# A fused attention and two-MLP kernel on one NeuronCore: first pair in native float32, shared transpose copies, sums on GpSimd, a new order

## The chip, the cores and the metric

The kernel runs on one core of a Trainium2 chip. The metric is the device time of one execution in microseconds (us), the median of several runs; lower is better. The engines are TensorE (PE for its matmuls, PEld for its weight loads), VectorE (DVE), ScalarE (ACT), GpSimd (POOL) and SyncE (SP, which issues every DMA of this kernel, in the order of its queue).

## What is computed

Block-causal attention over 4 batches, 8 heads, 576 positions and 64 columns a head; its output is the token matrix (2304 x 512) of two MLPs in a row.

```python
scores = scale * np.matmul(q, k.transpose(0, 1, 3, 2))
mask = block_i >= block_j            # blocks of 64 positions
attn = np.exp(scores - max); attn = attn / (sum + 1e-09)
x = np.matmul(attn, v)               # -> 2304 x 512
a = x @ w1;  b = x @ w2
x = (a * b @ w3) @ w_out             # 512 -> 1024 -> 1024 -> 512
h = x @ w_in                         # 512 -> 2048
out = np.where(h > 0, h, np.exp(np.minimum(h, 0)) - 1) @ w_out2
```

## The kernel before

**Precision.** Most matmuls run in three passes over operands that are split into a rounded part and a remainder (type fp32r; `PASSES` has the three combinations). A few run in native float32; the trace records each of these as two MATMUL rows. The weights come as 64-bit words, and `convert` makes float32 of each unit of 128 x 512 on ACT, DVE and POOL (L425 to L461), in four input buffers (`cr`).

**Stages.** First, attention for 16 pairs of heads (`attention(n, ...)`, n = 0 to 15) runs beside the product of w3 and w_out (`w_product`: 64 float32 matmuls `wps` of 128 x 512), which needs 24 converted units (`full`). Then `block2` multiplies the tokens with w1, w2 and that product (`a`, `b`, `y`); its matmuls mix with the attention of the later pairs. Last, `part_h` and `part_o` do the second MLP by a seven-product scheme (`hx hy hz`, `ox oy oz`); their weights come back from DRAM through a ring of three buffers `win` and one of four `wout`.

**One pair.** q and k are loaded into `raw` and split: ACT rounds (L570, L573), POOL and DVE make the remainders (L578, L583). For each of four groups of 128 queries (`group(g, seq)`) PE makes the scores `s` of both heads (L631, and L637 for the mask in the first four pairs), DVE takes the maxima (L652), ACT the exponentials with their sums (L657), PE transposes them into a bank `t` (L667), and ACT or DVE copies the bank to `pt` (`evac`, L521 or L522). `last_block` does the last 64 queries with a block-diagonal q (`qb`). `pv` multiplies with v (`o`, L757). `recip` adds up the sums and inverts them on DVE (L780 to L784); they go through DRAM (`scr`, `rr`) and POOL normalizes (L811). The score banks are 0, 1 and 2; `t` and `o` take turns in banks 3 and 4.

**Order.** `Plan.add` collects every operation with an engine, a guessed duration, a priority and its dependencies; `Plan.run` puts them in order by these guesses, and each engine then works through its list in that order. `TURNS` overrides the priority of some operations by their number. Until the first `wps` product, `filler` puts matmuls on a spare bank (`spare`, L1486) into gaps that the plan expects on PE.

Of the kernel before, what the change touches and what calls it, by code (L numbers as in the profile page):

```python
# [20 lines left out]
P = 128  # L21
WHOLE = 0
# [4 lines left out]
WO_PRIO = -3000.0  # L27
# [7 lines left out]
KP = 4  # L35
# [112 lines left out]
class Ring:  # L148
# [11 lines left out]
    def next(self):  # L160
        k = self.k % self.n
        self.k += 1
        self.last[k] = Buf(self.pool, self.tags[k], self.base, self.shape, self.dtype, self.last[k], self.gate)
        return self.last[k]
# [124 lines left out]
def attention_moe_moe2(  # L289
# [236 lines left out]
    def attention(n, first_op):  # L526
# [77 lines left out]
        def nm(c):  # L604
            return st()[:, c:c + 1]
# [938 lines left out]
```

## Time and profile before

| | before |
|---|---|
| median of 3 runs (lowest to highest) | 909.37 us (908.26 to 911.37) |
| the profiled execution: time, span | 908.46 us, 906.7 us |
| PE busy | 887.0 us (98%) |
| PEld busy | 785.4 us (87%) |
| DVE busy | 731.5 us (81%) |
| ACT busy | 504.9 us (56%) |
| POOL busy | 555.4 us (61%) |
| DMA | 186.15 MB, mean 205 GB/s |

The span runs from the first to the last instruction on the core; the 1.76 us between it and the execution's time lie outside. Matmuls are pipelined and their ends are modelled, so PE can count as busy while it makes less headway than it could.

### The profile page before, as it was taken

The numbers are of one execution on the slowest core, as the hardware profiler recorded it, in microseconds if no ns is written. First come the engines' busy times: TensorE is split into PE (matmuls) and PEld (weight loads), VectorE is DVE, ScalarE is ACT, GpSimd is POOL, SyncE is SP. The second block draws the span as 40 slices with busy tenths as digits, with TensorE's granted clock in tenths as the row PEclk, the third lists the DMA queues.
The fourth block names the chain that finished last, engine by engine and source line by source line (L and its number), as shares of the span: only waits on it lengthen the run. The fifth ranks groups of instructions, "written<-read, shape, count | busy, mean of one in ns | idle before, by whom it ended". The sixth has DMA issues, their size and how long they took to land.

```text
span 906.7 us, 15391 instructions
## 1 busy us (share of the span) xinstructions
PE 887.0 (98%) x5268; PEld 785.4 (87%) x5268; DVE 731.5 (81%) x1406; ACT 504.9 (56%) x1168; POOL 555.4 (61%) x529
## 2 busy tenths in 40 slices
PE   8899999999999999999999999999999999999998
PEld 3455568877788779999999999999999999999997
DVE  7998898798667675778898778788877788987896
ACT  6778876776556653435454554545634555444561
POOL 6666976454322223698898882138976178842796
PEclk9999999999999999999999999999999999999999
DMA  8765544554222105888567865877688776788666
GB/s 286 234 216 171 189 155 132 179 166 150 90 66 67 55 27 184 260 263 259 179 224 246 315 209 155 254 235 255 232 270 268 259 260 228 250 275 300 223 211 216
DMA packets 100750, 186.15 MB, mean 205 GB/s; under 512 B 8512, under 2 KB 50496, under 8 KB 100672
## 3 DMA queue, kind: packets, MB, share of 16 engines
q1 hardware_dynamic: 100672, 185.18, 61.8%
q8 instruction: 41, 0.67, 0.3%
q14 instruction: 37, 0.30, 0.1%
HBM read 147.85 MB, written 37.30 MB: 204 GB/s over the span
## 4 chain that ended last, share of the span: by engine, by line
PE 78%; DMA 8%; DVE 7%; POOL 2%; ACT 2%; issue 2%; SPq 1%; ACTq 0%; POOLq 0%; DVEq 0%
PE b L941 11%; PE a L941 10%; PE y L902 10%; PE hx L1192 8%; PE ox L1270 6%; PE hz L1192 5%; PE hy L1192 5%; PE o L757 4%; PE oz L1270 4%; PE oy L1270 4%; PE s L631 3%; PE t L667 3%; DMA win<-wsi 3%; PE wps L827 2%; DMA cr<-w 2%
## 5 line engine op out<-in xcount | busy, mean ns | idle before, releaser
L902 PE MATMUL y<-g,slab_lo 128*128 128x384 f32 x576 | 114.9, 340 | 0.4 <-DVE xy L925 0.3
L941 PE MATMUL b<-xs,slab_lo 128*128 128x384 f32 x576 | 111.3, 338 | 0.0
L941 PE MATMUL a<-xs,slab_lo 128*128 128x384 f32 x576 | 110.8, 337 | 0.0
L941 PEld LDWEIGHTS b<-xs,slab_lo 128*128 128x128 f32 x576 | 99.9, 188 | 0.7 <-DVE af L958 0.4
L941 PEld LDWEIGHTS a<-xs,slab_lo 128*128 128x128 f32 x576 | 99.9, 188 | 0.5 <-issue 0.5
L902 PEld LDWEIGHTS y<-g,slab_lo 128*128 128x128 f32 x576 | 99.0, 188 | 1.3 <-PE y L902 0.6
L1192 PE MATMUL hx<-sy,win 128*128 128x384 f32 x432 | 86.9, 335 | 0.1
L657 ACT ACTIVATE p<-s,st 128x256 f32<-128x256 f32 (+3 forms) x128 | 67.4, 529 | 29.0 <-DVE st L652 23.2
L1192 PEld LDWEIGHTS hx<-sy,win 128*128 128x128 f32 x432 | 75.7, 188 | 0.9 <-DVE ga L1074 0.4
L1270 PE MATMUL ox<-sp,wout 128*128 128x384 f32 x372 | 73.2, 334 | 0.0
L863 POOL TENSOR_TENSOR g<-af,g 128x384 fp32r<-128x384 f32 x48 | 53.8, 1125 | 26.4 <-ACT g L860 26.0
L652 DVE TENSOR_REDUCE st<-s 128x1 f32<-128x256 f32 (+3 forms) x128 | 61.6, 488 | 5.8 <-PE s L637 2.5
L1270 PEld LDWEIGHTS ox<-sp,wout 128*128 128x128 f32 x372 | 65.3, 188 | 0.0
L827 PE MATMUL wps<-full,full 128*128 128x512 f32 x128 | 60.8, 602 | 2.1 <-POOL full L455 1.9
L1192 PE MATMUL hz<-sy,win 128*128 128x384 f32 x288 | 58.0, 335 | 3.3 <-DMA win<-wsi 3.3
L1192 PE MATMUL hy<-sy,win 128*128 128x384 f32 x288 | 57.8, 335 | 0.2 <-DMA win<-wsi 0.2
L667 PE MATMUL t<-ident,p 128*128 128x128 f32 x320 | 54.3, 282 | 2.9 <-ACT p L657 2.0
L667 PEld LDWEIGHTS t<-ident,p 128*128 128x128 f32 x320 | 37.0, 140 | 22.5 <-ACT p L657 8.2
L432 ACT ACTIVATE ct<-cr 128x512 f32<-128x512 f32 x59 | 39.9, 677 | 29.4 <-POOL wt L455 13.6
L425 ACT ACTIVATE cr<-cr 128x512 int32<-128x512 uint32 x72 | 48.6, 681 | 11.9 <-DMA cr<-w 7.9
L1192 PEld LDWEIGHTS hz<-sy,win 128*128 128x128 f32 x288 | 50.4, 188 | 4.3 <-DMA win<-wsi 4.3
L757 PE MATMUL o<-pt,v 128*64 128x320 f32 (+4 forms) x448 | 52.7, 367 | 1.0 <-ACT pt L521 1.0
(175 smaller groups left out, 2135.1 us busy)
## 6 DMA issues: line engine op xcount, KB each, us to landing
wout<-wso SPq DMA_DIRECT2D x84, 512.0 KB
cr<-w SPq DMA_DIRECT2D x48, 512.0 KB
win<-wsi SPq DMA_DIRECT2D x24, 1024.0 KB
win<-wsi SPq DMA_DIRECT2D x24, 768.0 KB
cr<-w3T SPq DMA_DIRECT2D x16, 512.0 KB
wsi<-wh SPq DMA_DIRECT2D x8, 896.0 KB
wsi<-wt SPq DMA_DIRECT2D x8, 896.0 KB
wso<-wh SPq DMA_DIRECT2D x8, 896.0 KB
```

The lines of the kernel that those rows point to most:

```text
L425: nc.scalar.activation(out=low, in_=low.bitcast(U32), func=AF.Copy, scale=2.0**-29)
L432: nc.scalar.activation(out=t().bitcast(F32), in_=words()[1].bitcast(F32), func=AF.Abs)
L652: nc.vector.tensor_reduce(out=nm(c), in_=s()[:, 0:nk], axis=AX.X, op=ALU.max, negate=True)
L657: lambda s=s, c=c, p=p: nc.scalar.activation(out=p()[:, 0:nk], in_=s()[:, 0:nk], func=AF.Exp, bias=nm(c), scale=1.0, accum_out=sm(c)),
L667: nc.tensor.transpose(d[:, j, :], p()[:, j * P:(j + 1) * P], ident)
L757: nc.tensor.matmul(o()[D * h:D * h + D, lo:cols], lhsT=vt()[0:kn, j, D * h:D * h + D], rhs=p, start=(j == 0), stop=(j == last),)
L827: nc.tensor.matmul(ps(), lhsT=a[:, j, :], rhs=bb, start=(j == 0), stop=(j == KF - 1))
L863: lambda: nc.gpsimd.tensor_tensor(out=g()[:, 1, :], in0=src(), in1=g()[:, 0, :].bitcast(F32), op=ALU.subtract),
L902: nc.tensor.matmul(ps()[:, 0:T2], lhsT=w[:, a, n * P:(n + 1) * P], rhs=gs[m]()[:, c, :], start=(m == ms[0] and q == 0), stop=(m == ms[-1] ...
L941: nc.tensor.matmul(ps()[:, 0:T2], lhsT=w[:, a, u, k, :], rhs=xs()[:, k, c, :], start=(k == 0 and q == 0), stop=(k == KD - 1 and q == 2),)
L1192: nc.tensor.matmul(bk()[:, 0:T3], lhsT=w[:, a, k, :], rhs=s_(c), start=(first and k == 0 and i == 0), stop=(k == 1 and i == 2), skip_group ...
L1270: nc.tensor.matmul(to[n]()[:, 0:T3], lhsT=w[:, a, n * P:(n + 1) * P], rhs=sp(c), start=(first and q == 0 and i == 0), stop=(q == KP - 1 an ...
```

## The change

Five things change together.

1. `WHOLE` goes from 0 to 1: pair 0 is loaded straight into its q and k tiles in two column pieces (256 and 320), k is scaled piece by piece, and its scores are native float32 matmuls, one a head and group; its q for the last block has a buffer of its own, `qw`. It is also placed first on SP and PE, ahead of all weight products.
2. In groups 0 and 1 (`BOTH`) the transposes of the two heads go into one bank, and one copy moves both.
3. In `recip` the addition of the two last sums and of 1e-9 move from DVE to POOL, an operation of their own (`sums_of`) ahead of the reciprocal.
4. In the very last product of `part_o` the two halves of the output no longer alternate (`split_end`), and the filler before PE's first operation is counted at 0.45 us instead of 0.29 us.
5. `TURNS` is a new table, so the order changes on all engines throughout.

```diff
-WHOLE = 0
+WHOLE = 1
+BOTH = 2
-WO_PRIO = -3000.0
+WO_PRIO = -2499.995
...
-    4: -2505.56, 9: -100000.02, 22: -9857.07, 23: -997.98, 36: -3035.53, 41: -2498.87, 65: -2417.38, 69: -2499.99,
+    4: -10173.49, 5: -10172.92, 6: -10173.47, 7: -10173.5, 8: -2499.97, 24: -2452.67, 40: -9872.36, 56: -2400.0,
...
-                self.filler(int((t - free[e] - 0.6) / 0.29))
+                self.filler(int((t - free[e] - 0.6) / (0.29 if free[e] else 0.45)))
...
+        halves = (slice(0, 256), slice(256, S)) if whole else ()
...
+            for c, cs in enumerate(halves):
+                add(
+                    "SP", 0, lambda cs=cs: nc.sync.dma_start(out=f32(x, 0)[:, cs], in_=src[b, hp][:, cs]),
+                    w=[(x, 0, c)], prio=pr + 0.001 * c, nbytes=P * (cs.stop - cs.start) * 4,
+                )
...
+            if both:
+                t2 = turn("to", (3, 4), "t")
...
-                t = turn("to", (3, 4), "t")
+                t = t2 if both else turn("to", (3, 4), "t")
+                t0 = nk * h if both else 0
...
+                if both and h:
+                    evac(
+                        2 * nk, lambda pt=pt: pt()[:, :, 0:g + 1, q0:q0 + P],
+                        lambda t=t: t()[:, 0:2 * nk].rearrange("p (h j q) -> p h j q", h=2, q=P),
+                        [(t, 0), (t, 1)], [(pt, 0, g), (pt, 1, g)], pg,
+                    )
...
         def recip():
             a = st()
-            nc.vector.tensor_tensor(out=a[:, 16:17], in0=a[:, 16:17], in1=a[:, 21:22], op=ALU.add)
-            nc.vector.tensor_scalar_add(a[:, 12:21], a[:, 12:21], 1e-9)
             nc.vector.reciprocal(a[:, 32:41], a[:, 12:21])
...
+        def sums_of():
+            a = st()
+            nc.gpsimd.tensor_tensor(out=a[:, 16:17], in0=a[:, 16:17], in1=a[:, 21:22], op=ALU.add)
+            nc.gpsimd.tensor_scalar_add(a[:, 12:21], a[:, 12:21], 1e-9)
...
-                        prio=1e5 + 1000 * (j + 1) + 34 * (KP * x + q) + 17 * n, lag=LAG, kind="big",
+                        prio=1e5 + 1000 * (j + 1) + 34 * KP * x + (70 * n + 17 * q if split_end else 34 * q + 17 * n),
```

Three places show how the order moves. The first is the head of SP's queue, that is, what is loaded first. Before (`cr` are weights to convert, `raw` the q and k of a pair, `v` its values):

```order
L464 DMA cr_129<-wo 128x512
L464 DMA cr_131<-w3T 128x512
L464 DMA cr_129<-w3T 128x512
L464 DMA cr_131<-wo 128x512
L548 DMA v_145<-vt 128x4x128
L539 DMA raw_151<-kT 128x576
L539 DMA raw_151<-qT 128x576
```

Now, with the lines of the changed program:

```order
L550 DMA q_130<-qT 128x320
L550 DMA k_132<-kT 128x256
L550 DMA q_130<-qT 128x256
L471 DMA cr_142<-w3T 128x512
L550 DMA k_132<-kT 128x320
L471 DMA cr_153<-w3T 128x512
L555 DMA raw_157<-kT 128x576
L555 DMA raw_157<-qT 128x576
```

The pieces of the first pair's q and k stand ahead of all weights but two units; the second pair's q and k have moved up as well.

The second is the head of PE's list. Before, after 36 fillers:

```order
L1486 MATMUL spare<-mk 128x512
L827 MATMUL wps_226<-full_168,full_182 128x512
L827 MATMUL wps_237<-full_168,full_182 128x512
L631 MATMUL s_244<-k_228,q_234 128x256
L631 MATMUL s_246<-k_228,q_234 128x256
```

Now, after six fillers:

```order
L651 MATMUL s_168<-k_132,q_130 128x128
L651 MATMUL s_170<-k_132,q_130 128x128
...
L697 MATMUL t_185<-ident,p_179 128x128
L651 MATMUL s_187<-k_132,q_130 128x256
L651 MATMUL s_189<-k_132,q_130 128x256
...
L697 MATMUL t_185<-ident,p_182 128x128
```

Scores and transposes of the first pair stand ahead of the weight products; the first `wps` now stands behind the score products of the second pair's third group. Seven more fillers stand among the pair's operations. The two transposes write one bank, `t_185`.

The third is the end of PE's list, the last product `oy` in its two halves. Before:

```order
L1270 MATMUL oy_9816<-sx_9616,wout_9840 128x384 x3
L1270 MATMUL oy_9824<-sx_9616,wout_9840 128x384 x3
...
L1270 MATMUL oy_9816<-sx_9710,wout_9860 128x384 x3
L1270 MATMUL oy_9824<-sx_9710,wout_9860 128x384 x3
```

Now:

```order
L1312 MATMUL oy_9719<-sx_9537,wout_9738 128x384 x6
L1312 MATMUL oy_9703<-sx_9537,wout_9738 128x384 x3
L1312 MATMUL oy_9719<-sx_9582,wout_9758 128x384 x6
L1312 MATMUL oy_9703<-sx_9537,wout_9738 128x384 x3
L1312 MATMUL oy_9703<-sx_9582,wout_9758 128x384 x6
```

One half now ends nine matmuls ahead of the other instead of three.

## Rows read from the trace of the kernel before

**Rows 1.** Busy time by stage: us, then busy time and instructions of each engine.

```profile
24.00:71.20 47.20, 43.20 (x229) 23.31 (x228) 44.45 (x98) 35.35 (x89) 28.23 (x28) 1.00 0.70 232
71.20:119.90 48.70, 48.47 (x229) 25.22 (x227) 41.97 (x85) 38.76 (x92) 38.08 (x33) 1.00 0.56 179
119.90:344.00 224.10, 221.86 (x1552) 179.69 (x1551) 170.63 (x458) 141.33 (x408) 93.92 (x102) 1.00 0.33 104
344.00:625.00 281.00, 280.72 (x1624) 279.02 (x1624) 224.89 (x356) 135.49 (x252) 191.24 (x168) 1.00 0.72 235
625.00:850.00 225.00, 221.25 (x1265) 218.53 (x1264) 185.97 (x320) 114.79 (x248) 142.09 (x134) 1.00 0.77 263
850.00:907.00 57.00, 52.10 (x298) 51.15 (x296) 46.02 (x62) 24.04 (x51) 46.81 (x41) 0.99 0.63 203
```

**Rows 2.** Timeline of the first 40 us: start, us, instruction, idle before it.

```profile
0.74 0.39 SPq L464 DMA_DIRECT2D cr<-wo  x1
...
1.98 9.28 PE L1486 MATMUL spare<-mk 128*128 128x512 bf16 x36 [1.98 <-POOL mk L1337]
...
4.51 0.15 PEld L1486 LDWEIGHTS <-mk 128*128 128x128 bf16 x1 [0.28 <-issue]
4.71 0.43 DVE L434 TENSOR_SCALAR ct<-cr 128x512 int32<-128x512 int32 x1 [4.71 <-DMA cr<-wo]
...
4.83 5.93 PEld L1486 LDWEIGHTS <-mk 128*128 128x128 bf16 x28 [0.17 <-issue]
...
6.35 0.68 ACT L432 ACTIVATE ct<-cr 128x512 f32<-128x512 f32 x1 [0.94 <-DMA cr<-w3T]
...
11.41 1.10 PE L827 MATMUL wps<-full,full 128*128 128x512 f32 x2
...
13.91 0.38 PE L631 MATMUL s<-k,q 64*128 64x256 f32 x2
...
39.68 2.42 PE L757 MATMUL o<-pt,v 128*64 128x320 f32 x20
```

**Rows 3.** The chain that ended last: start, us, what; two pieces of PE's work.

```profile
66.71 2.35 PE o L757 x20
...
79.26 3.44 PE wps L827 x8
```

**Rows 4.** Copies of transposes in the first 346 us, by form: busy us, mean ns, idle.

```profile
L521 ACT COPY pt<-t 128x512 f32<-128x512 f32 x18 | 10.5, 586 | 4.9 <-PE t L727 3.4 <-PE t L667 1.6
...
L521 ACT COPY pt<-t 128x256 f32<-128x256 f32 x21 | 7.4, 372 | 7.2 <-PE t L667 7.2
...
L521 ACT COPY pt<-t 128x128 f32<-128x128 f32 x25 | 6.3, 268 | 9.5 <-PE t L667 9.5
```

**Rows 5.** The instructions on st (sums): ns min/median/max, first and last start.

```profile
L780 DVE TENSOR_TENSOR st<-st x16: 146/158/374, 41.8 to 339.4; 128x1 f32<-128x1 f32 x16
L781 DVE TENSOR_SCALAR st<-st x16: 173/173/1210, 41.9 to 339.6; 128x9 f32<-128x9 f32 x16
L786 POOL MEMSET st<- x16: 111/118/1107, 2.6 to 295.3; 128x23 f32 x16
```

**Rows 6.** PE's waits: us in total, times, longest.

```profile
PE hz L1192 <- DMA win<-wsi: 3.3, 3, 1.6
PE s L631 <- ACT p L716: 2.0, 3, 1.0
```

**Rows 7.** The chain that ended last: loads of win in it, issue and us.

```profile
632.37 6.25 DMA win<-wsi
...
653.10 7.73 DMA win<-wsi
```

**Rows 8.** Timeline of the last 7 us.

```profile
899.81 2.59 PE L1270 MATMUL oy<-sx,wout 128*128 128x384 f32 x14
...
902.61 1.07 DVE L1074 TENSOR_TENSOR ob<-oy,ot 128x384 f32<-128x384 f32 x2 [1.52 <-DMA out<-ob]
```

**Rows 9.** Exponentials in the first 346 us, by form: busy us, mean ns.

```profile
L657 ACT ACTIVATE p<-s,st 128x256 f32<-128x256 f32 x32 | 15.2, 475 | 9.7 <-DVE st L652 9.4
```

More of the change, by code (lines that the diff above doesn't have):

```diff
@@ L158, in share, with next @@
         return r
-    def next(self):
+    def next(self, dtype=None):
         k = self.k % self.n
         self.k += 1
-        self.last[k] = Buf(self.pool, self.tags[k], self.base, self.shape, self.dtype, self.last[k], self.gate)
+        self.last[k] = Buf(self.pool, self.tags[k], self.base, self.shape, dtype or self.dtype, self.last[k], self.gate)
         return self.last[k]
@@ L510, in attention_moe_moe2 @@
     mb = p1.tile([P, D], BF16, name="mb")
-    ev = [0]
+    qw = p1.tile([P, P], F32, name="qw") if WHOLE else None
     def act_us(n, sbuf=False):
@@ L530, in attention @@
         whole = n < WHOLE
-        qs, ks, vt = qs_r.next(), ks_r.next(), v_r.next()
+        whole_type = F32 if whole else None
+        qs, ks, vt = qs_r.next(whole_type), ks_r.next(whole_type), v_r.next()
         raw = None if whole else raw_r.next()
         rr, st, rs, scr = rr_r.next(), st_r.next(), rs_r.next(), scr_r.next()
-        q8 = qb[n % 2]
+        q8 = qw if whole else qb[n % 2]
         S_BANKS = (0, 1, 2)
+        halves = (slice(0, 256), slice(256, S)) if whole else ()
         def load(x, part, src):
-            to, key = ((lambda: f32(x, 0)), (x, 0)) if whole else ((lambda: raw()[:, part, :]), (raw, part))
-            add("SP", 0, lambda: nc.sync.dma_start(out=to(), in_=src[b, hp]), w=[key], prio=pr, nbytes=P * S * 4)
+            for c, cs in enumerate(halves):
[3 more added lines that the diff above has]
+                )
+            if not whole:
+                add(
+                    "SP", 0, lambda: nc.sync.dma_start(out=raw()[:, part, :], in_=src[b, hp]), w=[(raw, part)],
+                    prio=pr, nbytes=P * S * 4,
+                )
+        load(ks, 1, kT)
         load(qs, 0, qT)
-        load(ks, 1, kT)
         def load_v(j):
@@ L555, in f32, with scale_k @@
         def f32(x, part):
-            return x()[:, part, :].bitcast(F32)
-        def scale_k(eng):
+            a = x()[:, part, :]
+            return a if whole else a.bitcast(F32)
+        def scale_k(eng, cs):
             if eng is nc.scalar:
-                nc.scalar.activation(out=f32(ks, 1), in_=f32(ks, 0), func=AF.Copy, scale=SCALE)
+                nc.scalar.activation(out=f32(ks, 1)[:, cs], in_=f32(ks, 0)[:, cs], func=AF.Copy, scale=SCALE)
             else:
-                nc.vector.tensor_scalar_mul(f32(ks, 1), f32(ks, 0), SCALE)
+                nc.vector.tensor_scalar_mul(f32(ks, 1)[:, cs], f32(ks, 0)[:, cs], SCALE)
         if whole:
-            add(
-                "ACT", 0.67, lambda: scale_k(nc.scalar), r=[(ks, 0)], w=[(ks, 1)], prio=pr,
-                ways=[("DVE", 0.45, lambda: scale_k(nc.vector), True)],
-            )
+            for c, cs in enumerate(halves):
+                cn = cs.stop - cs.start
+                add(
+                    "ACT", act_us(cn, True), lambda cs=cs: scale_k(nc.scalar, cs), r=[(ks, 0, c)], w=[(ks, 1, c)], prio=pr,
+                    ways=[("DVE", 0.15 + cn * 0.00052, lambda cs=cs: scale_k(nc.vector, cs), True)],
+                )
         else:
@@ L592, in q_last @@
                 if whole:
-                    nc.gpsimd.tensor_copy(q8.bitcast(F32)[p0:p0 + D, 0, p0:p0 + D], f32(qs, 0)[p0:p0 + D, 512:576])
+                    nc.gpsimd.tensor_copy(q8[p0:p0 + D, p0:p0 + D], f32(qs, 0)[p0:p0 + D, 512:576])
                 else:
@@ L597, in attention, with q_keys, k_keys @@
         add(
-            "POOL", 0.6, q_last, r=[(qs, 0)] if whole else [(qs, 0), (qs, 1)], w=[("qb", n % 2)], prio=pr + 1, port=True
+            "POOL", 0.6, q_last, r=[(qs, 0, 1)] if whole else [(qs, 0), (qs, 1)], w=[("qb", 2 if whole else n % 2)], prio=pr + 1, port=True
         )
-        q_keys = [(qs, 0)] if whole else [(qs, 0), (qs, 1)]
-        k_keys = [(ks, 1)] if whole else [(ks, 0), (ks, 1)]
+        def q_keys(g):
+            return [(qs, 0, g // 2)] if whole else [(qs, 0), (qs, 1)]
+        def k_keys(g):
+            return [(ks, 1, c) for c in range(1 + g // 2)] if whole else [(ks, 0), (ks, 1)]
         def nm(c):
@@ L610, in sm, with two_banks @@
             return st()[:, 12 + c:13 + c]
+        def two_banks():
+            return [turn("s", S_BANKS, "s") for _ in range(2)]
         def group(g, seq):
@@ L616, in group @@
             w = nk if whole else max(256, nk)
-            added = n < ADDED
-            sb = [turn("s", S_BANKS, "s") for _ in range(2)]
+            added, both = n < ADDED, g < BOTH
+            sb = two_banks()
             def scores():
@@ L642, in group @@
                 "PE", (4 * w / 2390 if whole else 3 * w * COL) + (0.28 if added else 0.21), scores,
-                r=[*q_keys, *k_keys, "mask"], w=[*sb], prio=pg, kind="s",
+                r=[*q_keys(g), *k_keys(g), "mask"], w=[*sb], prio=pg, kind="s",
             )
+            if both:
+                t2 = turn("to", (3, 4), "t")
             for h in range(2):
@@ L661, in group, with transposes @@
                 )
-                t = turn("to", (3, 4), "t")
-                def transposes(p=p, t=t):
-                    d = t().rearrange("p (j q) -> p j q", q=P)
+                t = t2 if both else turn("to", (3, 4), "t")
+                t0 = nk * h if both else 0
+                def transposes(p=p, t=t, t0=t0):
+                    d = t()[:, t0:t0 + nk].rearrange("p (j q) -> p j q", q=P)
                     for j in range(g + 1):
                         nc.tensor.transpose(d[:, j, :], p()[:, j * P:(j + 1) * P], ident)
-                add("PE", 0.109 * (g + 1), transposes, r=[p, "ident"], w=[t], prio=pg, kind="t")
+                add("PE", 0.109 * (g + 1), transposes, r=[p, "ident"], w=[(t, h)], prio=pg, kind="t")
                 pt = pts[g // 2]
                 q0 = P * (g % 2)
-                evac(
-                    nk, lambda h=h, pt=pt: pt()[:, h, 0:g + 1, q0:q0 + P],
-                    lambda t=t: t().rearrange("p (j q) -> p j q", q=P)[:, 0:g + 1, :],
-                    [t], [(pt, h, g)], pg,
-                )
+                if both and h:
[3 more added lines that the diff above has]
+                        [(t, 0), (t, 1)], [(pt, 0, g), (pt, 1, g)], pg,
+                    )
+                elif not both:
+                    evac(
+                        nk, lambda h=h, pt=pt: pt()[:, h, 0:g + 1, q0:q0 + P],
+                        lambda t=t: t().rearrange("p (j q) -> p j q", q=P)[:, 0:g + 1, :],
+                        [(t, h)], [(pt, h, g)], pg,
+                    )
         def last_block(seq):
@@ L680, in last_block @@
             kw = S // 2
-            sb = [turn("s", S_BANKS, "s") for _ in range(2)]
+            sb = two_banks()
             p = p_r.next()
@@ L687, in scores @@
                         nc.tensor.matmul(
-                            sb[g]()[:, 0:kw], lhsT=q8.bitcast(F32)[:, 0, :], rhs=f32(ks, 1)[:, g * kw:(g + 1) * kw],
+                            sb[g]()[:, 0:kw], lhsT=q8, rhs=f32(ks, 1)[:, g * kw:(g + 1) * kw],
                             start=True, stop=True,
@@ L699, in last_block @@
                     "PE", (4 * kw / 2390 if whole else 3 * kw * COL) + 0.09, scores,
-                    r=[("qb", n % 2), *k_keys], w=[sb[g]], prio=pg, kind="qb",
+                    r=[("qb", 2 if whole else n % 2), *k_keys(3)], w=[sb[g]], prio=pg, kind="qb",
                 )
@@ L709, in last_block @@
             add(
-                "DVE", 0.16, lambda: nc.vector.tensor_tensor(out=nm(10), in0=nm(8), in1=nm(9), op=ALU.min),
+                "DVE", 0.19, lambda: nc.vector.tensor_tensor(out=nm(10), in0=nm(8), in1=nm(9), op=ALU.min),
                 r=[(st, "nm", 8), (st, "nm", 9)], w=[(st, "nm", 10)], prio=pg, port=True,
@@ L786, in attention @@
         add("POOL", 0.15, lambda: nc.gpsimd.memset(st()[:, 41:64], 0.0), w=[(st, "rest")], prio=pr)
-        add("DVE", 0.85, recip, r=[(st, "rest"), *((st, "sm", c) for c in range(10))], w=[(st, "rs"), rs], prio=pr + 6, port=True)
+        def sums_of():
+            a = st()
+            nc.gpsimd.tensor_tensor(out=a[:, 16:17], in0=a[:, 16:17], in1=a[:, 21:22], op=ALU.add)
+            nc.gpsimd.tensor_scalar_add(a[:, 12:21], a[:, 12:21], 1e-9)
+        add("POOL", 0.4, sums_of, r=[(st, "sm", c) for c in range(10)], w=[(st, "total")], prio=pr + 6, port=True)
+        add("DVE", 0.42, recip, r=[(st, "rest"), (st, "total")], w=[(st, "rs"), rs], prio=pr + 6, port=True)
         def keep_sums(b):
@@ L1243, in part_o @@
             first = name in ("p1", "p6", "p5")
+            split_end = j == NP * N3 - 1 and name == "p3"
             for q in range(KP):
@@ L1277, in part_o @@
                         "PE", 3 * T3 * COL + 0.01, mm, r=[(wb, 0), *spk], w=[to[n]],
-                        prio=1e5 + 1000 * (j + 1) + 34 * (KP * x + q) + 17 * n, lag=LAG, kind="big",
+                        prio=1e5 + 1000 * (j + 1) + 34 * KP * x + (70 * n + 17 * q if split_end else 34 * q + 17 * n),
+                        lag=LAG, kind="big",
                     )
@@ L1342, in start_qb, with start_qw @@
             nc.gpsimd.memset(q.bitcast(F32), 0.0)
+    def start_qw():
+        nc.gpsimd.memset(qw, 0.0)
     add("POOL", 0.6, start, w=["ident"], prio=-1e5)
     add("POOL", 0.8, start_mask, w=["mask"], prio=-1e5)
+    if WHOLE:
+        add("POOL", 0.25, start_qw, w=[("qb", 2)], prio=-1e5)
     add("POOL", 0.7, start_qb, w=[("qb", 0), ("qb", 1)], prio=-1e5)
```

144 rows, old and new, of the table TURNS are left out of this document.

## Prediction

> **What bounds the kernel now.** First the busy time by stage. PE is busy nearly always, so the question is how much headway it makes. From 344 to 625 us it runs 1624 matmuls of 384 columns in 281.0 us, 173 ns each [rows 1]; nothing is lost there and no edit can help. At 173 ns the 1265 matmuls from 625 to 850 need 218.8 us and lose 6.2; the 298 after 850 need 51.6 of the 56.7 us up to the span's end and lose 5.1.
>
> The rest is lost in front. I take as PE's own work what its operations need at the shortest distance to the next start that the trace shows between neighbours of the same kinds. A weight product is two records at 0.43 us, 0.86 us (eight records last 3.44 us [rows 3]); a pair of heads is about 9.55 us: the large `o` 2.35 us [rows 3], the small one 0.80, scores 2.7 to 2.9, the last block's scores 0.96, 25 transposes of 0.109. All 64 products and four pairs are done at 120.0 us. That is 64 x 0.858 = 54.9, plus 4 x 9.55 = 38.2, plus 4.7 for changes of kind and the fifth pair's first scores: 97.8 us of own work, so 22.2 us are lost. From there to 344 us another 7.5 are lost by the same count (216.6 us of own work in 224.1), in many waits of 0.1 us and a few near 1 us.
>
> Of the 22.2 us, 11.4 pass before the first product: until then PE runs 36 fillers, because the first weights land at 4.7 and 6.35 us and must be converted [rows 2]. The first pair's scores start at 13.91 us. Between 24.0 and 71.2 us DVE is busy 44.45 of 47.20 us (94%) and PE makes 41.1 us of own work, 87%; from 71.2 to 120.0 it makes 47.3 of 48.8, 97%, with DVE at 86% [rows 1]. So the first 71 us are shared: DVE's conversions and maxima hold PE as much as PE holds itself.
>
> **The change part by part.** *First pair.* The loads move to the head of SP's queue. The first load of 512 KB, issued at 0.74 us, has landed by 4.71, the third instruction's data by 6.35 [rows 2], so 512 KB cost some 1.6 us and the way there 2.4. Three pieces of 128 to 160 KB are then there at about 4.4 us, k's first piece is scaled, and scores can start near 4.6 us, when the six fillers end (1.98 + 6 x 0.43). Each float32 product takes four of PE's column times where three passes took three, so the pair's scores cost about 0.4 us more; ACT's two roundings and the splitting on POOL and DVE go. No float32 scores are in the trace; between nothing more than the old time and twice the old 3.7 us I take the ratio of the `wps` rows, 0.43 us for half of 512 columns.
>
> When is this pair done? Before, 25.8 us pass from its first score to its last `o` at 39.68 us [rows 2]. In them PE also makes 11 weight products (9.4 us) and 1.3 us of the second pair. Without those 15.1 us remain, so the last `o` starts at 19.7 us. Bounds: 13.8 us if PE alone set the pace (9.2 us of own work), 30.4 if the pair took as long as it does now.
>
> After that, 94.7 us of PE's own work remain up to the last product; the new order puts 24 matmuls of `block2` and more of the fifth pair ahead of it, 103.9 in all. Before, PE made 88.4 us of own work in the 96.0 us from 24.0 to 120.0, 92%. At that pace the last product ends at 19.7 + 102.8 = 122.5 us and 18.6 us are lost instead of 22.2: **3.6 us gained**. At 97% it is 117.4 us and 8.7 gained; at 87% 128.4 and 2.3 lost. I take the middle pace because the work that DVE, ACT and POOL must do by then is the same conversions as before.
>
> *Sums on POOL.* DVE is rid of 16 x (0.158 + 0.173) us, 5.3 in all. The longest of these took 1.21 us, seven times the median, without more work to do [rows 5]. [...] POOL has no such small sum in the trace; bounds for one are a memset of 23 columns at its median, 0.118 us, and at its longest, 1.107 [rows 5]; I take 0.15, near the first, 0.3 us for the two. POOL is busy 94 of 224 us after 120 [rows 1], and what now waits behind a sum on POOL is one conversion. The reciprocal is late by that; the way on goes through two DMAs, and the reader is far off. Within the pace above: 0.
>
> *Shared copies.* Two copies of 128 columns on ACT take 2 x 268 ns, one of 256 takes 372; two of 256 take 744, one of 512 takes 586 [rows 4]. So 0.16 us for each of 32, 5 us of ACT and DVE time over 344 us, and one bank is claimed less each time. The cost is that a bank is held from the first head's transposes to the second's. The second waits for its exponential, 0.475 us for 256 columns [rows 9], unless other work stands between them. I take 0: in the new list other products mostly stand there.
>
> *Order.* PE leaves the big matmuls for attention 60 times instead of 70, and each such leave costs about 0.1 us (a start 270 ns after a big one, not 173): with the float32 scores the own work of the whole program falls by **1.0 us**. From 120 to 344 us I keep the 7.5 us of loss. From 625 to 850 us PE waits on `win`: 3.3 us in front of `hz` [rows 6] and some 0.8 hidden in busy time, 4.1 of the 6.2. Loads on the chain took 6.25 to 7.73 us from issue to landing (four of them) [rows 7]. I counted PE's own work between the last use of a buffer and the first use of its next load: below 8 us for 18 of 48 `win` loads before, 9 now; the shortest are 5.2, 5.7 and four of 6.3 to 6.8 us. At a landing time of 6.5 to 7 us these wait 2.6 us together: **1.5 us gained**, between 4 and a loss of 3 if each landed as late as 7.7.
>
> *End.* The last evictions are two in a row, 902.61 to 903.68 us [rows 8]; with one half ready 1.56 us earlier one is left behind PE: **0.5 us gained**. If the output's DMAs, which now release the buffers at 902.5, hold the second too, it is 0.
>
> The sum: 3.6 + 1.0 + 1.5 + 0.5 = 6.6 us, a span of 900.1 and an execution of 901.9 us against the profiled 908.46. That execution lies 0.9 us below the median of the three runs, so I write 902.3.
>
> **The rivals.** *VectorE keeps the gain* (0.22). DVE starts at 4.71 us and is nearly full to 71 us; if it has no free time, PE's earlier start turns into later waits. For it: 94% busy. Against: the first pair leaves it more to do early. The 3.6 us are gone: 905.9 us.
>
> *PE runs freely* (0.15). With a whole pair in hand the products have no attention to wait for and the pace is the 97% of 71 to 120 us: 5.1 us more gain, 897.2 us.
>
> *A half clock* (0.08). Fillers start 0.43 us apart until 4.8 us and 0.21 apart after (28 in 5.93 us) [rows 2]: 512 columns at 1.2 and at 2.4 GHz, though the column of the granted clock reads 1.00. PE had been busy without a break since 1.98 us when it rose. Now only 13 fillers run, with gaps in the first pair. [...] At half rate the pair's 9.2 us double; about half would lie under other engines' work: 4.6 us lost, 906.9 us.
>
> *Shared banks hold PE* (0.07), the slower case. PE takes its list in order. If the second head's transposes stand ahead of what could run, each of the 32 shares costs up to 0.475 us: 15 us, 910 to 917. Against: PE waited for exponentials 2.0 us in all before the change in scores [rows 6]. From some 20 of 32 exposed the change ends slower.
>
> *Loads of the end fall short* (0.06). Nine `wout` loads in the last 25 us have 5.2 to 5.7 us; before, ten had 6.2 there and none waited. If 6.2 is needed, some 5 us are lost: 907.3.
>
> **How the numbers follow.** The forecast has 0.42, with 899.5 to 905 us for itself. 0.3%, 2.7 us, is what a measurement of this kernel can tell from no change: below 906.6 is faster, above 912.1 slower. The forecast, free PE, most of the first rival and half of the clock and load cases are faster, 0.80; slower are only the worse shared-bank case and the mishaps left, 0.06; same 0.14. The range from 895.5 to 908 leaves out the shared banks and the ends of the free pace.
>
> **What would show it.** The first scores near 4.6 us and the first pair's last `o` near 20 us; the last weight product near 122 us; fewer than 3.3 us of waits on `win`; the last two evictions 1.5 us apart. It is wrong if fillers after 5 us still start 0.43 us apart, if PE waits on `p` in front of `t` for more than 5 us, or if PE loses more than 7.5 us between the last weight product and the end of the last pair.

## The result and the profile after

The changed kernel takes 899.02 us (median of 4, 898.50 to 900.77) where the kernel before takes 910.37 us (4 runs beside it): a ratio of 0.9882, 95% interval 0.9857 to 0.9907. Two more measurements of the same instructions gave 0.9895 (0.9872 to 0.9917) and 0.9893 (0.9872 to 0.9913). So it is 1.05 to 1.2% faster, 9.6 to 10.7 us; 7.1 were forecast. The profiled execution has a span of 897.7 us, 9.0 less than before.

The profile's page, busy time with its share of the span and instructions:

```profile
span 897.7 us, 15305 instructions
...
PE 883.1 (98%) x5235; PEld 785.0 (87%) x5235; DVE 711.7 (79%) x1360; ACT 502.0 (56%) x1138; POOL 569.7 (63%) x572
```

By stage, in the columns of [rows 1]. The cuts answer to those of before: the 64th weight product ends at 121.0 us (120.0 before), the last pair's large `o` starts at 352.5 (344.0).

```profile
24.00:71.20 47.20, 45.91 (x270) 26.59 (x267) 44.31 (x94) 38.68 (x98) 31.51 (x35) 1.00 0.72 231
71.20:121.00 49.80, 48.34 (x169) 25.01 (x168) 45.48 (x87) 32.69 (x66) 34.36 (x31) 1.00 0.64 203
121.00:352.50 231.50, 229.86 (x1601) 190.58 (x1600) 165.10 (x431) 143.72 (x392) 107.55 (x129) 1.00 0.34 105
352.50:633.50 281.00, 279.99 (x1606) 275.38 (x1606) 224.00 (x355) 140.92 (x266) 207.16 (x189) 1.00 0.74 246
633.50:850.00 216.50, 215.05 (x1237) 214.00 (x1236) 180.46 (x311) 108.82 (x234) 139.76 (x131) 1.00 0.78 264
850.00:898.00 48.00, 44.02 (x251) 43.00 (x249) 36.69 (x54) 20.18 (x42) 39.61 (x33) 0.99 0.59 197
```

PE is busier in the first row (97% of 47.2 us, 92% before) with DVE as full as it was. The fourth row is the surprise: in the same 281.0 us PE makes 1606 matmuls where it made 1624 before, 18 x 173 ns = 3.1 us lost in a stage that had no loss. The fifth row answers to 625 to 850 us: 216.5 us for 1237 matmuls, 214.0 at 173 ns, 2.5 us lost instead of 6.2.

PE's timeline (start, us, instruction, idle before it), to be held against [rows 2]:

```profile
1.96 2.74 PE L1534 MATMUL spare<-mk 128*128 128x512 bf16 x6 [1.96 <-POOL mk L1380]
5.07 0.79 PE L651 MATMUL s<-k,q 64*128 64x128 f32 x4 [0.36 <-DMA q<-qT]
...
9.79 0.66 PE L697 MATMUL t<-ident,p 128*128 128x128 f32 x4
...
20.94 2.42 PE L794 MATMUL o<-pt,v 128*64 128x320 f32 x20
...
25.18 1.88 PE L868 MATMUL wps<-full,full 128*128 128x512 f32 x4
...
96.47 14.86 PE L868 MATMUL wps<-full,full 128*128 128x512 f32 x34 [1.46 <-DVE slab_lo L882]
...
118.25 2.74 PE L868 MATMUL wps<-full,full 128*128 128x512 f32 x6
```

The first pair is through 18.7 us earlier than before (39.68), and the first weight product stands behind it. What PE waits for now, against [rows 6] (us in total, times, longest):

```profile
PE wps L868 <- DVE slab_lo L882: 1.5, 1, 1.5
PE t L697 <- ACT p L686: 1.3, 4, 0.5
PE hz L1233 <- DMA win<-wsi: 1.2, 3, 0.8
...
PE hy L1233 <- DMA win<-wsi: 0.5, 1, 0.5
```

The waits on `win` are 1.7 us in all, 3.5 before. The end of the chain that ended last, against the span's last us in [rows 8]:

```profile
890.11 4.18 PE oy L1312 x24
894.28 0.02 issue
894.31 0.56 DVE ob L1115
```

One eviction follows PE. From PE's end to the span's end it is 3.45 us (894.27 to 897.72), 4.27 before. And the sums on POOL, against [rows 5] (ns min/median/max):

```profile
L824 POOL TENSOR_TENSOR st<-st x16: 182/191/737, 18.8 to 343.3; 128x1 f32<-128x1 f32 x16
L825 POOL TENSOR_SCALAR st<-st x16: 242/252/692, 19.0 to 343.5; 128x9 f32<-128x9 f32 x16
```

0.44 us for the two at the median, 0.3 forecast.

### The profile page after: what moved, and what is told of

Read it like the earlier page. It is cut to its first block, busy times and chain, and to the rows that moved or that the text cites. A ratio compares the mean times of both kernels' runs of the same rounds, so it can differ in the third digit from the quotient of the medians.

```text
span 897.7 us, 15305 instructions
## 1 busy us (share of the span) xinstructions
PE 883.1 (98%) x5235; PEld 785.0 (87%) x5235; DVE 711.7 (79%) x1360; ACT 502.0 (56%) x1138; POOL 569.7 (63%) x572
## 4 chain that ended last, share of the span: by engine, by line
PE 74%; DVE 9%; DMA 8%; POOL 4%; ACT 2%; issue 2%; SPq 0%; POOLq 0%; ACTq 0%
PE y L943 9%; PE a L982 9%; PE b L982 9%; PE ox L1312 8%; PE hx L1233 7%; PE hz L1233 5%; PE hy L1233 5%; PE oy L1312 5%; PE oz L1312 5%; PE o L794 4%; PE t L697 3%; PE s L658 3%; DMA win<-wsi 3%; DVE ct L453 2%; DMA cr<-w 2%
## 5 line engine op out<-in xcount | busy, mean ns | idle before, releaser
L686 ACT ACTIVATE p<-s,st 128x128 f32<-128x128 f32 (+3 forms) x128 | 67.3, 529 | 32.9 <-DVE st L681 29.2
L1312 PE MATMUL ox<-sp,wout 128*128 128x384 f32 x372 | 75.1, 334 | 0.0
L681 DVE TENSOR_REDUCE st<-s 128x1 f32<-128x128 f32 (+3 forms) x128 | 61.8, 488 | 10.6 <-PE s L664 7.3
L868 PE MATMUL wps<-full,full 128*128 128x512 f32 x128 | 58.8, 598 | 1.5 <-DVE slab_lo L882 1.5
L1106 POOL TENSOR_TENSOR sp<-sum,sp 128x384 fp32r<-128x384 f32 x29 | 32.0, 1107 | 41.4 <-ACT sp L1105 41.3
L459 POOL TENSOR_TENSOR ct<-ct,cr 128x512 int32<-128x512 int32 x28 | 39.7, 1419 | 25.8 <-DVE ct L453 15.1
L999 DVE TENSOR_TENSOR af<-b,af 128x384 f32<-128x384 f32 x48 | 26.6, 555 | 36.7 <-PE b L982 27.7
L439 ACT ACTIVATE ct<-cr 128x512 f32<-128x512 f32 x58 | 39.3, 677 | 28.5 <-POOL wt L462 17.1
L852 POOL TENSOR_TENSOR xy<-xy,rr 128x576 f32<-128x576 f32 x16 | 23.1, 1442 | 50.6 <-DMA rr<-scr 15.8
```

Source lines behind the costliest of these rows:

```text
L439: nc.scalar.activation(out=t().bitcast(F32), in_=words()[1].bitcast(F32), func=AF.Abs)
L459: nc.gpsimd.tensor_tensor(out=t(), in0=t(), in1=words()[0], op=ALU.add)
L681: nc.vector.tensor_reduce(out=nm(c), in_=s()[:, 0:nk], axis=AX.X, op=ALU.max, negate=True)
L686: lambda s=s, c=c, p=p: nc.scalar.activation(out=p()[:, 0:nk], in_=s()[:, 0:nk], func=AF.Exp, bias=nm(c), scale=1.0, accum_out=sm(c)),
L868: nc.tensor.matmul(ps(), lhsT=a[:, j, :], rhs=bb, start=(j == 0), stop=(j == KF - 1))
L1312: nc.tensor.matmul(to[n]()[:, 0:T3], lhsT=w[:, a, n * P:(n + 1) * P], rhs=sp(c), start=(first and q == 0 and i == 0), stop=(q == KP - 1 an ...
```

## The experiments

Edits of the change are undone one by one. So that an edit moves little but itself, the changed kernel's finished order (each operation's place and its engine) is written out as a list, and the next place whose inputs have been issued is issued next. An operation whose inputs now come later still moves back:

```
-        o.prio = TURNS.get(o.n, o.prio)
+            o.place, o.on = PLACE[self.k], ENG[ON[self.k]]
...
+        while ready:
+            place, n = heapq.heappop(ready)
+            o = self.ops[n]
```

The table has each kernel's median with its ratio to the kernel before on its chip, and from its profiled execution the start of the large `o` of the first, fourth and last pair, the start of the 64th weight product, and PE's end. The first four kernels run the same instructions up to the last product, and their traces differ by 2 to 3.6 us in the first four of these columns and by 6.2 in PE's end, so a single column says something only beyond that.

| kernel | median us | ratio (95%) | 1st `o` | 4th `o` | 64th product | 16th `o` | PE end |
|---|---|---|---|---|---|---|---|
| changed kernel | 899.02 | 0.9882 (0.9857 to 0.9907) | 20.9 | 82.7 | 120.0 | 352.5 | 894.3 |
| same_order | 903.18 | 0.9895 (0.9872 to 0.9917) | 22.2 | 83.8 | 123.5 | 354.6 | 899.5 |
| same_again | 901.66 | 0.9893 (0.9872 to 0.9913) | 23.5 | 84.5 | 121.8 | 354.1 | 898.7 |
| halves_by_turns | 900.11 | 0.9885 (0.9864 to 0.9907) | 21.0 | 82.4 | 120.0 | 351.8 | 893.3 |
| old_order | 914.20 | 1.0019 (1.0005 to 1.0033) | 41.7 | 112.9 | 121.1 | 346.9 | 905.6 |
| old_code | 912.83 | 1.0006 (0.9989 to 1.0022) | 24.9 | 88.5 | 125.6 | 366.4 | 907.9 |
| split_pair | 904.99 | 0.9917 (0.9895 to 0.9939) | 24.3 | 85.6 | 125.4 | 357.4 | 899.9 |
| whole_loads | 905.56 | 0.9936 (0.9915 to 0.9956) | 24.4 | 85.9 | 123.1 | 355.4 | 897.5 |
| own_copies | 908.52 | 0.9966 (0.9950 to 0.9983) | 23.0 | 85.8 | 124.6 | 364.7 | 907.0 |
| sums_on_dve | 900.57 | 0.9889 (0.9867 to 0.9911) | 21.8 | 84.7 | 122.7 | 357.0 | 898.8 |
| early_sub | 902.45 | 0.9902 (0.9877 to 0.9927) | 23.0 | 84.3 | 121.9 | 354.9 | 897.4 |
| early_sub7 | 902.37 | 0.9899 (0.9874 to 0.9924) | 23.1 | 86.0 | 123.2 | 355.3 | 897.8 |
| no_fillers | 902.74 | 0.9906 (0.9887 to 0.9925) | 24.5 | 87.0 | 124.6 | 357.0 | 898.3 |

same_order, old_order, old_code and split_pair ran on one chip; halves_by_turns, own_copies, sums_on_dve and whole_loads on a second; the last three and same_again on a third.

**The reference.** same_order:

> The changed kernel with its order of operations written out, so that nothing moves when an edit is undone; no edit is undone here. Every theory: 899.0 us (898.5 to 900.8), the last weight product of the front near 121.0 us, and each stage of PE within 0.5 us of the changed kernel's own trace. What differs between the two traces is the size below which a stage's time says nothing.

The order is the changed kernel's, row for row, and so is the ratio. The stages are not within 0.5 us, though: 3.6 us are missing at the 64th product. Where they went is under the clock, below.

**Order or code?** old_order keeps the new code and takes every place and engine from the kernel before (its 36 fillers too); old_code keeps the new order and undoes the four code edits.

> All code edits of the change, but every operation in the old kernel's order and on its engine (pair 0 behind the first weight products again). Theory A, that the gain in front is PE's earlier start and so belongs to the order: first product again near 11.4 us, some 20 to 22 us lost by the 64th product, win waits of some 3 us again, 906 to 909 us. Theory B, that the code (native float32, shared copies, sums on POOL) takes load off DVE and ACT and thereby lets PE run: 902 to 904 us, with less than 19 us lost by the 64th product.

> The new order, but all four code edits undone: pair 0 rounded and split as before (still loaded first), own banks and copies for both heads, sums on DVE, halves of the last product by turns. Theory A (the order carries it): 901 to 905 us; the first score some 2 us later than 5.07 us, the last output about 0.9 us later after PE's end, the rest kept. Theory B (the code carries it): 906 to 909 us.

Both theories fell. The new code in the old order is 0.2% slower than the kernel before; the old code in the new order is no different from it. Neither half is worth anything alone. In old_code the loss has a place: from the fourth pair's `o` to the last one 278.0 us pass, 270.9 in same_order. Undone one at a time (below, each against the reference on its chip), own copies cost 0.81% and the rounded first pair 0.22%, the other two edits nothing that can be measured: 1.03% of the 1.11% that old_code loses. So the new order gains nothing without the shared copies.

**Which edit the order needs.** First the bank and copy that two heads share (undone, each head's copy runs on the shared copy's engine):

```
-            added, both = n < ADDED, g < BOTH
+            added, both = n < ADDED, False
...
-                if both and h:
-                    evac(2 * nk, ...)
+                evac(nk, ..., place, at_eng and ENG[at_eng])
```

> The new order with one edit undone: in the groups of one and two blocks each head has its own bank and copy again (12 of the transposes move a few places back, where their bank is still held). The forecast's step: nothing lost or gained, within 1 us at the last pair's o. The rival, which the run with the old code speaks for (9 us more between the fourth and the sixteenth pair, PE's waits on copies 5.8 us): the shared bank frees a bank in time, and without it most of those 9 us are lost: 6 to 9 us later at the last pair's o, 906 to 911 us.

8.4 us more in the median than halves_by_turns on the same chip. The two profiled executions lie further apart, 13.6 us, since this one was the slowest of its twelve; the stage alone takes 278.9 us from the fourth to the last pair, 269.4 there. What PE waited for in it, from 80 to 370 us, first with own copies, then with shared ones (halves_by_turns):

```profile
PE t L896 <- ACT pt L726: 3.2, 9, 0.6
PE wps L1061 <- DVE slab_lo L1075: 1.9, 1, 1.9
PE t L966 <- ACT pt L726: 0.4, 1, 0.4
...
PE t L896 <- DVE pt L727: 0.3, 1, 0.3
```

```profile
PE wps L1032 <- DVE slab_lo L1046: 1.6, 1, 1.6
PE a L1146 <- ACT af L1158: 0.2, 1, 0.2
PE y L1107 <- ACT xy L1124: 0.2, 1, 0.2
PE t L861 <- ACT xy L692: 0.2, 1, 0.2
```

`t <- pt` is a transpose that waits until a copy has emptied its bank. With shared copies there is none of 0.2 us or more in this stage. The rival was right. The eleven such waits make 3.9 of the 9.5 us; 1.7 are a fall of the clock (below), and some 3 us stand in no wait that the view names. But the loss repeats from pair to pair. From the tenth pair's `o` to the last one the six distances between them are 0.45, 0.47, 1.35, 0.53, 0.49 and 0.51 us longer than in halves_by_turns, and in old_code 0.46, 0.43, 1.32, 0.46, 0.49 and 0.47; in same_order they differ by 0.02 at most. Nor is it the clock alone: the nine executions of own_copies with a mean granted clock of 1.000, which all six of halves_by_turns have, keep a median of 907.7 us.

Two things limit this. Twelve transposes moved back with the edit, and the engines of the copies were not chosen anew, so 8.4 us is the price of own banks in this order, not in any order.

The sums:

```
-            nc.gpsimd.tensor_tensor(out=a[:, 16:17], ...)
-            nc.gpsimd.tensor_scalar_add(a[:, 12:21], ...)
+            nc.vector.tensor_tensor(out=a[:, 16:17], ...)
+            nc.vector.tensor_scalar_add(a[:, 12:21], ...)
```

> The new order with one edit undone: the two small sums of each pair run on DVE again, at the same place. The forecast's step: nothing, within 0.5 us at the last pair's o. The rival: DVE is 5 us busier in the first 345 us and queues in front of PE's maxima, 1 to 3 us later at the last pair's o.

0.9889 beside 0.9885: nothing that can be measured. In its one trace the last pair is 5.2 us later than in halves_by_turns, but that execution was the slowest of its six (904.1 us; the others 897.3 to 901.9), so the later `o` does not show the edit.

The first pair in two experiments: first rounded and split as before, its two loads and its roundings at the places of the pieces:

```
-WHOLE = 1
+WHOLE = 0
+EARLY_PAIR = 1
```

> The new order with one edit undone: pair 0 is loaded first but in two loads, rounded on ACT twice and split on POOL and DVE, three passes. The forecast's step: the first score comes near 7.2 us instead of 5.07 (load of 288 KB, two roundings of 0.7, one split of 1.4 us), the first pair's last o 1.5 to 2 us later, and about that much is still missing at the 64th product: 900.5 to 901 us. The rival, VectorE sets the pace of the front: less than 0.5 us missing at the 64th product, 899 to 899.5 us.

Then in native float32, but not in pieces:

```
-        halves = (slice(0, 256), slice(256, S)) if whole else ()
+        halves = (slice(0, S),) if whole else ()
```

> The new order with one edit undone: pair 0 stays in native float32, but k and q come in one load each and k is scaled in one piece. The forecast's step (the first piece brings the first score forward): the first score 1 to 1.5 us later than with the pieces, the first pair's o 0.5 to 1 us later, and less than that left at the 64th product. The rival: the scores of the larger groups waited for the second pieces anyway, and nothing is left at the first pair's o.

split_pair is 0.2% slower than same_order on its chip (1.8 us), with intervals that overlap; the first `o` comes 2.2 us later and the 64th product 1.9, which is the forecast's step in size. Part of it is the clock, which rose for good only by 15.3 us there, by 11.0 in same_order. Its scores start at 5.63 us and stop for DVE's split:

```profile
5.63 0.39 PE L826 MATMUL s<-k,q 64*128 64x256 f32 x2 [0.94 <-ACT k L762]
7.15 0.50 PE L826 MATMUL s<-k,q 64*128 64x256 f32 x4 [1.13 <-DVE k L772]
```

whole_loads is 0.5% slower than halves_by_turns, and not for the reason forecast: its first score is at 4.63 us, 0.3 us earlier. The loss comes behind it, in the timeline of ACT and PE:

```profile
7.75 0.91 PE L818 MATMUL s<-k,q 64*128 64x384 f32 x2
...
8.75 0.67 ACT L596 ACTIVATE cr<-cr 128x512 int32<-128x512 uint32 x1 [2.10 <-DMA cr<-w3T]
...
10.00 0.47 ACT L853 ACTIVATE p<-s,st 128x256 f32<-128x256 f32 x1 [0.33 <-DVE st L848]
...
10.62 1.00 PE L818 MATMUL s<-k,q 64*128 64x384 f32 x1 [1.97 <-ACT p L853]
...
12.25 1.11 PE L864 MATMUL t<-ident,p 128*128 128x128 f32 x4
```

With whole loads the first weights land at 8.75 us instead of 7.08, and their conversion stands in ACT's and DVE's queues ahead of the first pair's second group. ACT waits 2.1 us for a weight and DVE 2.75, with the pair's work ready behind it, and PE's clock fell (below). The mean granted clock is 0.996 to 0.998 in five of its six executions, 1.000 in all of halves_by_turns, so the fall goes with this edit. So the pieces pay less by an early score than by an earlier landing of the weights that stand between.

**The very last product.** Its two halves by turns again, as PE's rows end (x3: three of them in a row):

```
-MATMUL oy_9719<-sx_9582 x6
-MATMUL oy_9703<-sx_9537 x3
-MATMUL oy_9703<-sx_9582 x6
+MATMUL oy_9703<-sx_9537 x3
+MATMUL oy_9719<-sx_9582 x3
+MATMUL oy_9703<-sx_9582 x3
+MATMUL oy_9719<-sx_9582 x3
+MATMUL oy_9703<-sx_9582 x3
```

> The new order and code with one edit undone: the two halves of the very last product alternate again. The forecast's step: the last two evictions follow each other without a pause after PE's end, and the span ends 0.5 to 0.7 us later behind PE's end than with the edit (3.45 us there). The rival, from the run with the old code: there the halves alternated too, and the last eviction ended 0.60 us after PE, as with the edit; what cost 0.7 us before was the wait for an output buffer. Then 3.4 to 3.6 us. Up to the last product this kernel is the changed one, so its trace is the reference on this chip for the other three.

The end of the chain with the halves by turns:

```profile
889.16 4.18 PE oy L1476 x24
893.34 0.02 issue
893.37 0.56 DVE ob L1279
```

3.47 us from PE's end to the span's end; 3.45 with the split. The split gains nothing. Before, the chain went through an output's DMA at 900.6 to 902.5 us and then two evictions; in the new order the buffer is free in time, with or without it. The other two runs agree: the old order with the split (old_order) still ends 4.14 us behind PE, with two evictions in a row behind a DMA, and the new order without it (old_code) 3.58.

**The wait at 96 us, and the clock.**

> The changed kernel with its order written out, nothing undone, once more, as the reference on this chip for the three beside it. 0.988 to 0.990 of the kernel before. PE waits 1.4 to 2.4 us for one subtraction on DVE near 96 us; where it waits 2.3 us or so, the products after it should again be seen at 0.85 us between records instead of 0.43 (the half clock) for some 3 us, where it waits 1.6 us or less, not.

early_sub moves one row of DVE: the subtraction that frees the bank runs ahead of two passes of a conversion. early_sub7 has a seventh filler besides; no_fillers has none.

```
 TENSOR_SCALAR ct<-ct
+TENSOR_TENSOR slab_lo<-wps,slab_lo
 TENSOR_SCALAR cp<-ct
 SCALAR_TENSOR_TENSOR ct<-cr,cp
-TENSOR_TENSOR slab_lo<-wps,slab_lo
```

> One row moved on DVE: the subtraction for which PE waits near 96 us runs ahead of the two passes of a conversion (0.69 us each) that stand before it. Theory: the bank is free 1.3 us earlier, PE waits under 1 us there, never long enough to fall to half clock, and the 64th product comes 1 us earlier than in the fast executions and up to 3.5 us earlier than in those that fell; 1 to 2 us less in the median than the changed kernel. Rival: DVE's conversions that now come 0.7 us later are themselves what PE waits for next, and the 64th product keeps its time.

> As with the moved subtraction, and a seventh filler ahead of the first scores, so that PE has no pause from 1.96 us until they start near 5 us. Theory of the clock: it rises near 4.8 us as in the kernel before, the scores of 256 columns already start 0.21 us apart instead of 0.32, and the first pair's o comes 0.3 to 0.5 us earlier. Rival: PE waits for maxima and exponentials in the first pair, and a faster clock there moves nothing: within 0.2 us.

> The changed kernel without its 13 fillers and nothing else changed. The half-clock rival of the forecast: without work before 4.9 us and in the gaps of the first pair PE stays at half clock through most of the first pair (transposes 0.218 us apart until some 16 us, as in the runs with the old code and with whole loads), the first pair's o comes 2 to 4 us later, and 1 to 3 us of it are left at the 64th product. Otherwise the clock rises by 10 us as with the fillers and the first pair's o is within 0.5 us.

In early_sub the wait at 96 us is gone, 50 records run in a row, and then PE stands for 1.28 us at the next operation that needs DVE:

```profile
89.56 21.93 PE L1032 MATMUL wps<-full,full 128*128 128x512 f32 x50
112.77 1.33 PE L1146 MATMUL b<-xs,slab_lo 128*128 128x384 f32 x6 [1.28 <-DVE slab_lo L1046]
```

The same wait in same_again is 1.25 us at 98 us, and the 64th product starts at 121.8 and 121.9 us. The rival was right that the time stays: the wait moved, though to another subtraction (`slab_lo`) and not to a conversion. The median did not improve (0.9902 beside 0.9893), and no version tried beats the changed kernel.

Without fillers the ratio is 0.9906, 0.1% from same_again and within the intervals. The transposes of the first pair ran at half clock until some 16 us there, as that rival had it, and the 64th product starts 2.8 us later than in same_again. But the seventh filler did not bring the clock up, against its theory, and in same_again, with all fillers, it was half too:

```profile
11.86 1.11 PE L861 MATMUL t<-ident,p 128*128 128x128 f32 x4
```

Four transposes in 1.11 us; 0.66 us in the changed kernel's own trace (above, 9.79 us).

## Why the prediction held, point by point

The time lies in the stated range, 0.5 us below the band that the forecast kept for itself (899.5 to 905 us). The accounts of the two traces bear out its mechanism in front; one term was far off, and an opposite error hid it. Between the profiled executions 6.6 us were forecast and 9.0 measured. (The last step of the sum, from 901.9 to 902.3 us, adds 0.4 where its reason gives 0.9.) Lost PE time before and after, counted as in the prediction:

| stage | lost before, us | lost after, us | gained | forecast |
|---|---|---|---|---|
| to the 64th product | 22.2 | 17.1 | 5.1 | 3.6 |
| to the last pair's `o` | 7.5 | 4.8 | 2.7 | 0 |
| next 281 us | 0 | 3.1 | -3.1 | 0 |
| to 850 us | 6.2 | 2.5 | 3.7 | 1.5 |
| rest | 5.1 | 4.3 | 0.8 | 0.5 |
| PE's own work | | | 0 | 1.0 |

These make 9.2 us of the 9.0 between the two spans.

**First pair: right.** The first score came at 5.07 us (4.6 forecast; the piece of q landed 0.36 us after the fillers), the last `o` at 20.94 (19.7), the last product ended at 120.99 (122.5). The four column times of a float32 product are what the weight products show: 0.86 us for 512 columns, against 0.216 us for a filler's 512. From 20.94 us on PE made its 94.7 us of own work in 100.05, 95%, between the 92% taken and the 97% of the rival in which PE runs freely. Part of that is luck of the execution: in same_order and same_again the 64th product starts 3.6 and 1.8 us later, in halves_by_turns at the same time, and over the four the gain is 3.7 us, near the 3.6. That it comes from the first pair's early place is read from this account; no run moves that pair alone.

**Shared copies: the step that failed.** "I take 0" should have been the largest term. In the new order the edit is worth 8.4 us in the median (0.9966 against 0.9885). The count of copy time, 5 us of ACT and DVE, was not the price; the named part of the price is a bank that comes free for the next transposes. The rival that shared banks hold PE did not occur: waits of `t` on `p` are 1.3 us, in four. The sum held by luck: it kept the 7.5 us of loss of this stage, 4.8 were measured with shared copies, and with own ones the new order would lose some 13 (4.8 + 8.4, an estimate), so what the order costs here and what the copies give back nearly cancel. That the old order was made for own banks and hid their cost fits old_order and old_code, and was not tested further.

**Order.** The old order with the new code gains nothing, so the table and the code are one change; a sum over parts, as the prediction made it, cannot say so. The 1.0 us of own work is not there: the stages less their losses are 865.8 us before and 865.9 after. A count that ends with the start of PE's last unbroken stretch, three matmuls from the end before and nine after, would make it (6 x 0.173 = 1.04 us); no view on record shows the count itself.

**The stage without loss.** "Nothing is lost there and no edit can help" holds for before only. From the 1500th to the 2000th matmul of 384 columns 89.0 to 90.5 us pass in all twelve traces with the new order and 86.7 and 86.9 in the two with the old one (500 x 173 ns are 86.5). So the loss goes with the order. Which of its rows cause it was not tried; the waits of 0.2 us and more that the trace names there, on `ga`, `cp`, `g` and `win`, add to 1.0 us.

**`win` loads: right, and larger.** 1000 matmuls on, from the 2000th to the 3000th, take 174.8 to 177.0 us in the new order and 178.0 and 178.9 in the old. The rival of the loads of the end did not occur: PE's one wait on `wout` is 0.2 us.

**End: right size, wrong cause.** halves_by_turns shows that the split gives nothing; the buffers, which the prediction named as what could hold the gain back, are what gave it.

**Sums on POOL: right.** No difference is measured (0.9889 beside 0.9885). Single sums stay long on POOL: the longest took 0.737 and 0.692 us, with medians of 0.191 and 0.252. The one of 0.737 us ran beside two conversions on DVE and ended 0.05 us after the second (160.03 and 160.08 us); before, DVE's sum of 1.21 us ended 0.03 us after a conversion on POOL (108.81 and 108.84). What held these two was not shown.

**VectorE keeps the gain: partly.** early_sub shows this rival's mechanism at the end of the front: DVE frees banks and slabs just in time, and a wait removed at 96 us is paid at 112.

**A half clock: it occurs.** It had 0.08 and 4.6 us. It comes in some executions and not in others, and costs some 2 us each time, as follows. The prediction's sign for being wrong, fillers still 0.43 us apart after 5 us, is there in same_again (two at 12.77 and 13.19 us), and its ratio held all the same (0.9893): as a sign it was too strict.

## What to carry to other kernels

A new order and the code that it was made for are one change: each alone gave nothing here (1.0019, 1.0006), both together 1.1%; undo parts under a frozen order before saying what each is worth. Price a shared buffer by the wait that its freed twin removes, not by the copies saved. And here, with DVE 91% busy from 71 to 121 us, moving its row earlier for one waiter moved the wait to the next.

## What the runs showed of the hardware that was not expected

The same first 15 us of instructions ran at different clocks. Two transposes start 0.109 us apart at the higher level and 0.214 at the lower, two fillers 0.216 and 0.427 (a filler's 512 columns over these are 2.4 and 1.2 columns a ns; the prediction's GHz are that estimate). The column of the granted clock reads 1.00 in either case, because the trace's record of it begins with the first rise (at 4.72 us in the trace of before). With the 6 fillers in front, PE ran at the higher level by 7.0 us in the changed kernel's trace, in halves_by_turns, sums_on_dve and whole_loads, by 11.0 in same_order, and only by 14.9 us in same_again, early_sub and own_copies; with 7 fillers by 14.9 too, and without any after 16. From the first score to the first pair's `o` it took 15.9 to 17.0 us with the early rise (19.7 in whole_loads, which fell again) and 18.0 to 18.3 with the late one. Before, with 36 fillers in a row, it rose at 4.8 us [rows 2]; the same 36 in old_order, 10.57 us instead of 9.28, were at half clock until 7.3. The rise differs by 2.5 us between the two rows of 36 fillers and by 4 and 8 us with 6; what decides it among equal executions was not settled.

It also fell behind waits. In same_order PE waited 2.26 us at the place where the changed kernel waited 1.46, and then made 14 records of weight products in 7.97 us where 0.43 us each would be 6.0, with a granted clock of 0.79 from 98.0 to 106.3 us:

```profile
98.33 7.97 PE L1032 MATMUL wps<-full,full 128*128 128x512 f32 x14 [2.26 <-DVE slab_lo L1046]
```

split_pair (2.36 us) and own_copies (1.86) show the same there, whole_loads around its 1.97 us at 10.6 (granted clock 0.50 from 10 to 16 us), and old_order behind 1.92 us, where four transposes then took twice their time:

```profile
30.54 0.95 PE L958 MATMUL o<-pt,v 128*64 128x256 f32 x8 [1.92 <-ACT pt L692]
31.42 1.12 PE L861 MATMUL t<-ident,p 128*128 128x128 f32 x4
```

Waits of 1.46 to 1.62 us at the same place (changed kernel, halves_by_turns, no_fillers) were not followed by it, nor was one of 1.95 (sums_on_dve), and in no_fillers the granted clock is 0.50 from 23.8 to 27.1 us behind waits of only 1.09 and 0.53 us, so the length alone does not decide. In same_order the stretch from the fourth `o` to the 64th product is 2.5 us longer than in the changed kernel, 0.8 of it the wait itself. The fall reaches the total: the three executions of same_order with a mean granted clock of 0.997 or 0.998 take 904.2 us on average, the three at 1.000 take 902.3.
